# A spectral mix and an attention in one stream of matmuls: maxima ahead by more tiles, keys loaded by head, ones rows sent first

## The chip, the cores and the metric

The kernel runs on one core of a Trainium2 chip. Time is the device time of one execution in microseconds. Within the core, TensorE (PE) multiplies, VectorE (DVE), ScalarE (ACT) and GpSimd (POOL) do the work on vectors, and SyncE (SP) issues most of the copies between memories; POOL issues some too. Each engine takes its instructions in the order in which they are written, and stops at one whose inputs or outputs are not ready. PSUM is the memory into which PE writes, in eight places of 128 x 512 here.

## The reference, cut to what matters

The result mixes two branches row by row, 2048 rows of 512. Branch A is the real part of a two-dimensional Fourier transform, written as products with four given matrices. Branch B is attention with 32 heads of 16 columns.

```
g = sigmoid((x * gate_w).sum(-1))
a = x @ Wd_re.T;  b = x @ Wd_im.T
y = Ws_re @ a - Ws_im @ b
q, k, v = split(x @ wqkv)            # 32 heads of 16
o = softmax(q @ k.T / 4) @ v ;  B = o @ wo
out = g * y + (1 - g) * B
```

## The kernel before

Every float32 factor is split into a high and a low part, so that a product takes three matmuls. The heads are taken in 16 pairs; pair `p` has 32 units `u` (two halves of the queries by 16 blocks of keys), 512 units in all. For a pair, `qs` and `ks` hold q and k of head 0 in the lower 64 partitions and of head 1 in the upper 64, with rows left for a maximum (in `qs`) and for ones (in `ks`): the product of the two then gives the scores with the row's maximum already taken off. There are two `qs` and two `ks`, used by even and odd pairs.

Per unit, PE makes scores (`scores`, L787), ACT their exponentials (L788), PE the product with v (`pv`, L823, and `pv_last`, L804, for the last 16 units). Ahead of that the maxima are needed: `a_tile` makes a product of 128 queries by 512 keys (L247), and DVE takes its largest value (L249); after 64 of these per head a pair's maxima are done, and `m_parts` and `m_rows` write them into `qs`. Tiles are taken head by head: in each head tile `i` of pair `p` goes first over the keys' block 0, for eight blocks of queries (the low half), then over block 1, and so on.

PE works on 64 rows at once in either half, so most work goes in slots of two matmuls: one of branch A or of the projections in one half, one score or maximum in the other. The order of the slots is written out as patterns: `s` a score, `a` a maximum, `d` a product of the other branch alone, a capital letter a second one in the other half, `|` the end of a segment. A segment gives one head its scores, the next the other. At `|` the plan is run (`run_plan`): what was put down with `at(u, ...)` for units up to one beyond those whose values are done is issued there, among it the loads of q and k of the next pair. The segments are 24 THIN, 192 FULL, 2 TWELVE, 30 TEN and 8 at the end.

Before the segments come the projections, v, the imaginary part of A's first product, and then the first real rows, in `four`: four phases of 12 slots, with other work put in behind the slots of some `j` (`between`). There the first maxima are made: `maxima` in the imaginary stage (70 tiles per head, `LEAD`), and `first_tiles` in the stage of the first real rows. The lead is the number of tiles per head that are done when the segments begin; from then on scores and maxima go at the pace of the patterns.

What sets the order around the change: POOL's queue at the start (memsets of `ks`, `qs` and `vt`, and the copies of the rows of ones), SP's queue in the segments (loads of q, `load_q`, whose last copy clears rows of `qs` from a tile of zeros; loads of k in four blocks of 512 keys; copies of A's matrices, `craw`; y, o and r rows to and from memory), and the plan that says after which segment a load is issued.

Of the kernel before, what the change touches and what calls it, by code (L numbers as in the profile page):

```python
# [10 lines left out]
F32 = mybir.dt.float32  # L11
# [5 lines left out]
P = 128  # L17
S = 2048
D = 512
H = 32  # L20
DH = 16
NP = H // 2
KT = D // P
NT = S // P
UNITS = NP * 32
# [7 lines left out]
def mix_kernel(ctx: ExitStack, tc: tile.TileContext, xa_t, xa, wqkv, w_hid, w_seq, wo, gate_w, out):  # L33
# [5 lines left out]
    nc = tc.nc  # L39
# [9 lines left out]
    qk_d = [dram.tile([2, D, S], F32, name=f"qk{c}") for c in range(2)]  # L49
# [29 lines left out]
    def turn_of(kind):  # L79

        group = {"f": banks, "s": banks[:4], "a": [*banks[4:], psD], "r": banks[4:]}[kind]
        turns[kind] += 1
        pool = group[(turns[kind] - 1) % len(group)]
        return pool.tile([P, 512], F32, name="d" if pool is psD else "t")
# [20 lines left out]
    def staged(src):  # L105
        raw = st1.tile([P, D], F32, name="raw", bufs=RAW)
        nc.sync.dma_start(raw, src)
        return raw
# [94 lines left out]
    qs, ks = [None] * 2, [None] * 2  # L203
# [6 lines left out]

    PARTS = (0, 0, 1), (0, 1, 0)

    def load_rows(p, c, cols):


        t = (qs, ks)[c][p % 2]
        rows = slice(2 * p * DH, 2 * (p + 1) * DH)
        for i, v in enumerate(PARTS[c]):
            nc.sync.dma_start(t[i:P:4, cols].bitcast(F32), qk_d[c][v, rows, cols])

    def clear(t, rows, cols):
        dst = t[rows, cols].bitcast(F32).rearrange("r (n c) -> r n c", c=P)
# [3 lines left out]
    def load_q(p, cols):  # L226
        load_rows(p, 0, cols)
        if p > 1:
            clear(qs[p % 2], slice(3, P, 32), cols)
# [8 lines left out]
    def a_tile(i, h, ps=None):  # L238
        p, j = divmod(i, 64)
        n = 4 if p == NP - 1 and j >= 32 else 8  # L240
        k, j = divmod(j, 4 * n)
        kb, qt = divmod(j, n)
        qt += n * k
        if ps is None:
            ps = turn_of("a")
        r = slice(64 * h, 64 * h + 64)
        nc.tensor.matmul(ps, qs[p % 2][r, qt * P:(qt + 1) * P], ks[p % 2][r, kb * 512:(kb + 1) * 512],  # L247
                         start=True, stop=True)
        user = nc.vector.tensor_reduce(mx[p % 2][:, h, qt, kb:kb + 1], ps, AX.X, ALU.max)  # L249
        a_left[p, n, k] = a_left.get((p, n, k), 8 * n) - 1  # L250
        if not a_left[p, n, k]:
            deferred.extend((partial(m_parts, p, n, k), partial(m_rows, p, n, k)))
        return user
# [24 lines left out]
    ones = st1.tile([4, 2 * D], F32, name="hl", bufs=2)  # L278
    nc.gpsimd.memset(ones, 1.0)
    for i in range(2):  # L280
        nc.gpsimd.memset(ks[i].bitcast(F32), 0.0)
        (nc.gpsimd if i else nc.vector).memset(qs[i].bitcast(F32), 0.0)  # L282
        if i == 0:
            load_rows(0, 1, ALL)
            load_q(0, ALL)
            nc.gpsimd.memset(vt[:, :, :, 16:17], 1.0)
        for tb in range(2):
            nc.gpsimd.dma_start(ks[i][3:P:32, tb * 2 * D:(tb + 1) * 2 * D].bitcast(F32), ones)
    wos = [staged(wo[:, kt]) for kt in range(KT)]
    wrs = []  # L290
    a_next = 0
# [3 lines left out]
    def row_products(s, wh, wl):  # L295

        t = ab[s]
        for kt in range(KT):
            hi, lo = (t[:, v, kt * P:(kt + 1) * P] for v in range(2))
            yield from ((hi, wh[kt]), (hi, wl[kt]), (lo, wh[kt]))  # L300
# [24 lines left out]
    def maxima():  # L325

        nonlocal a_next
        users = [a_tile(a_next, h) for h in range(2)]
        a_next += 1
        return users[1]  # L330

    def four(ss, wh, wl, done, between=None):

        ps = [turn_of("s") for _ in ss]
        seen = None
        for phase, pair in enumerate(((0, 1), (2, 3), (1, 0), (3, 2))):
            guard, seen = seen, None
            both = [row_products(ss[c], wh, wl) for c in pair]
            for j in range(12):
                for half, c in enumerate(pair):  # L340
                    st, mv = next(both[half])
                    r = slice(64 * half, 64 * half + 64)
                    i = nc.tensor.matmul(ps[c], st[r], mv[r], start=phase < 2 and j == 0, stop=phase > 1 and j == 11)  # L343
                    if phase > 1 and j == 0:
                        tc.add_manual_dep(
                            i.ins, guard.ins.name,
                            mybir.DependencyInfo(mybir.DependencyClass.Sync, mybir.DependencyReason.DATA))
                if j in (((2, 7), (1, 5, 10), (3, 8), (1, 5, 10))[phase] if not between else (3, 8)):
                    user = between(phase, j) if between else maxima()
                    seen = seen or user  # L350
            if deferred:
                deferred.pop(0)()
            if phase > 1:
                for c in sorted(pair):
                    done(ss[c], ps[c])
# [55 lines left out]
    def bank(i=None):  # L411

        nonlocal now
        if i is None:
            i = min(range(7), key=lambda j: free[j])
        now = max(now, free[i] + 0.7)
        return i, banks[i].tile([P, 512], F32, name="t")

    def read_by(i, kind):

        nonlocal dve, act
        if kind == "a":
            dve = max(now + 2.0, dve) + 2.6
            free[i] = dve + 0.4
        else:
            act = max(now + 2.0, act) + 2.1
            free[i] = act + 0.5
# [345 lines left out]
    def scores(u, qb, h, ps=None):  # L773
        p, r = divmod(u, 32)
        hf, kt = divmod(r, 16)
        q0 = hf * 1024 + qb * 512
        if u >= UNITS - 16:

            blk, kt = divmod(kt, 8)
            q0, kt = 1024 + blk * 512, 2 * kt + qb  # L780
        if u not in pts:
            pts[u] = work.tile([P, 4, 512], F32, name="pt", bufs=4)
        if ps is None:
            i, ps = bank()
            read_by(i, "s")
        rr = slice(64 * h, 64 * h + 64)
        nc.tensor.matmul(ps, ks[p % 2][rr, kt * P:(kt + 1) * P], qs[p % 2][rr, q0:q0 + 512], start=True, stop=True)  # L787
        return nc.scalar.activation(pts[u][:, 2 * qb + h], ps, AF.Exp, bias=0.0, scale=DH ** -0.5)  # L788
# [94 lines left out]
    def at(u, f, *args):  # L883
        plan.setdefault(u, []).append(partial(f, *args))

    for p in range(2, NP):
        u = 32 * (p - 1)
        at(u - 14, load_q, p, LOW)
        for kb in range(4):
            at(u - 14 + 4 * kb, load_rows, p, 1, slice(kb * 512, (kb + 1) * 512))  # L890
        at(u - 2, load_q, p, HIGH)

    for hf in range(2):
        for ct in range(4):
            n = 3 if hf and ct == 3 else 4
# [28 lines left out]

    FULL = "s a s s a a s s a a s a s a a s |"
    THIN = "aS s a s a s s a s a s a a sA |"
    TWELVE = ("sA a s a s ^ s a s a s s a s |",) * 2
    TEN = "aA s s a s ^ s s s a a sS |", "a s a sS a ^ s s s s s aA |"

    def stream(h):  # L930

        return (
            iter([(u, qb, h) for u in range(UNITS) for qb in range(2)]),
            iter([(i, h) for i in range(lead, NP * 64)]),
        )

    streams = [stream(h) for h in range(2)]

    users, valued = [], 0
# [66 lines left out]
    def pairs():  # L1006

        for i in range(NT - 4):
            yield (THIN,) * 2, take(hid, 12)
        for i in range(2 * NT * 3):  # L1010
            yield (FULL,) * 2, take(seq, 16)
        for patterns, n in ((TWELVE, 1), (TEN, 15)):
            for i in range(n):
                yield patterns, take(both_first, 9)

# [13 lines left out]

    def first_tiles(phase, j):  # L1030

        if j == 3:
            user = scores(*next(streams[0][0]), turn_of("r"))
            a_tile(*next(streams[1][1]), turn_of("r"))
            return user
        for h in range(2):
            a_tile(*next(streams[h][1]), turn_of("r"))

    four(range(4), *wre, first_rows, first_tiles)
    free[:] = 0.0, 0.0, 4.0, 4.0, 1.0, 2.0, 3.0  # L1040
    hid, seq = real(), dft()
# [10 lines left out]
    for hf, qts in ((1, range(2)), (1, range(2, 5)), (1, range(5, 8)), (0, range(2))):  # L1052
        for half in range(2):
            ds = take(proj(hf, (3,), [held_bank] * (len(qts) - 1) + one, qts, half == 1), 9, False)
            if valued < UNITS - 12:
                pattern = TEN[half]
            else:
                pattern = "s s ^ s s s s s s |" if len(qts) < 3 else "s s ^ s s d s s s s |"
                if valued == UNITS - 2:
                    pattern = "s s s s d d |"  # L1060
            segment(pattern, half, ds, True, after.get(valued), False)
    assert not any(a_left.values())
    last_pair(last)
# [36 lines left out]
```

## Time and profile before

| | |
|---|---|
| median of 3 runs | 1669.23 us (1668.42 to 1669.26) |
| profiled execution | 1669.81 us |
| its span | 1667.9 us |
| PE busy | 1658.0 us, 99% |
| DVE busy | 1374.9 us, 82% |
| ACT busy | 1251.0 us, 75% |
| POOL busy | 753.4 us, 45% |

How to read it: the page lists busy time per engine, the span in 40 slices, the queues of copies, the chain of work that ended last, and the groups of instructions. A row of a timeline gives the start in us, the length in us, the engine, the line of the kernel, the operation, the tiles written and read, the shapes and a count; in brackets stands how long the engine was idle ahead of it, and what ended that. SPq and POOLq are copies at their issue; the length there is that of the issue and not of the transfer.

### The profile page before, as it was taken

Reading aid. Unit: us, or ns where it says so; the run is one execution under the profiler, and the core shown is the slowest. Engines: PE = TensorE matmul, PEld = TensorE weight load, DVE = VectorE, ACT = ScalarE, POOL = GpSimd, SP = SyncE. Lnnn points to the kernel's source line nnn. Section 1 sums busy time; section 2 is a strip of 40 time slices with the busy share of each in tenths; the row PEclk is TensorE's granted clock in tenths of the full one; section 3 lists DMA queues with packets and bytes.
Section 4 is the critical chain, followed back from the end, with each engine's and each line's share of the span. In section 5 each row is a group of like instructions: output and inputs, shape, how many; then the busy total and the mean of one; then the engine's idle time right before and its main releaser. Section 6 shows DMA issues by size and latency. Waiting matters only on the chain.

```text
span 1667.9 us, 34971 instructions
## 1 busy us (share of the span) xinstructions
PE 1658.0 (99%) x13170; PEld 984.6 (59%) x13170; DVE 1374.9 (82%) x2283; ACT 1251.0 (75%) x2486; POOL 753.4 (45%) x813
## 2 busy tenths in 40 slices
PE   9999999999999999999999999999999999999998
PEld 7878866655555555555555555555555555555554
DVE  5459988888888888888888888888888888877786
ACT  5212188887777788877777788877778788799995
POOL 0223643544454455544444465554545566333331
PEclk9999999999999999999999999999999999999999
DMA  9953301122221224222127224322222333451114
GB/s 295 342 156 132 151 21 38 29 59 60 71 70 51 63 80 130 73 65 65 54 76 263 79 84 122 95 76 67 71 65 68 92 97 117 149 194 43 26 48 134
DMA packets 90176, 165.65 MB, mean 99 GB/s; under 512 B 21056, under 2 KB 22472, under 8 KB 88856
## 3 DMA queue, kind: packets, MB, share of 16 engines
q1 hardware_dynamic: 85368, 162.63, 31.2%
q8 instruction: 104, 1.70, 0.4%
q0 software_dynamic: 4352, 0.39, 0.2%
q14 instruction: 64, 0.52, 0.1%
q10 hardware_dynamic: 288, 0.39, 0.1%
HBM read 107.73 MB, written 54.52 MB: 97 GB/s over the span
## 4 chain that ended last, share of the span: by engine, by line
PE 98%; DVE 0%; POOL 0%; DMA 0%; issue 0%; SPq 0%; DVEq 0%; ACT 0%
PE d L456 37%; PE t L823 28%; PE t L247 12%; PE t L787 9%; PE t L343 5%; PE t L93 2%; PE t L92 2%; PE t L91 2%; PE t L804 1%; PE t L456 1%; DMA ks<-qk 0%; PE t L161 0%; PE t L183 0%; DVE mx L249 0%; DVE yp L648 0%; PE t L733 0%
## 5 line engine op out<-in xcount | busy, mean ns | idle before, releaser
L249 DVE TENSOR_REDUCE mx<-t 128x1 f32<-128x512 f32 x2013 | 1253.2, 683 | 226.8 <-PE t L247 192.3
L788 ACT ACTIVATE pt<-t 128x512 f32<-128x512 f32 x2048 | 1033.5, 632 | 10.5 <-PE t L787 9.3
L787 PE MATMUL t<-qs,ks 64*128 64x512 f32 x2048 | 728.7, 408 | 0.4 <-DVE mx L249 0.2
L247 PE MATMUL t<-ks,qs 64*128 64x512 f32 x2013 | 675.6, 399 | 1.6 <-POOL qs L282 1.6
L456 PE MATMUL d<-xab,ch 64*128 64x512 f32 x2016 | 656.5, 400 | 0.0
L823 PE MATMUL t<-pt,vt 128*32 128x512 f32 x3968 | 477.1, 598 | 0.0
L456 PEld LDWEIGHTS d<-xab,ch 64*128 64x128 f32 x2016 | 357.8, 184 | 142.2 <-issue 98.1
L247 PEld LDWEIGHTS t<-ks,qs 64*128 64x128 f32 x2013 | 359.8, 184 | 84.2 <-ACT pt L788 55.9
L787 PEld LDWEIGHTS t<-qs,ks 64*128 64x128 f32 x2048 | 367.0, 184 | 71.3 <-DVE mx L249 40.8
L456 PE MATMUL d<-xab,cl 64*128 64x512 f32 x1008 | 403.4, 400 | 0.0
L838 POOL TENSOR_TENSOR osum<-osum,oe 128x512 f32<-128x512 f32 x217 | 279.6, 1289 | 161.7 <-ACT oe L832 153.8
L832 ACT COPY oe<-t 128x512 f32<-128x512 f32 x217 | 127.4, 587 | 215.5 <-PE t L823 213.8
L823 PEld LDWEIGHTS t<-pt,vt 128*32 128x32 f32 x3968 | 103.6, 109 | 232.1 <-issue 148.7
L401 POOL CAST ch<-craw 128x512 fp32r<-128x512 f32 x126 | 77.3, 613 | 348.4 <-PE t L787 322.7
L456 PEld LDWEIGHTS d<-xab,cl 64*128 64x128 f32 x1008 | 185.8, 184 | 72.3 <-issue 50.3
L402 POOL TENSOR_TENSOR cl<-craw,ch 128x512 fp32r<-128x512 f32 x126 | 162.3, 1288 | 10.2
L270 POOL DMA_DIRECT2D qs<-mt x132 | 73.6, 562 | 90.4 <-DVE mt L266 80.1
L456 PE MATMUL d<-wo_hl,o_hl 64*128 64x512 f32 x288 | 75.3, 395 | 0.0
L456 PE MATMUL d<-wre,xab 64*128 64x512 f32 x288 | 70.3, 389 | 0.0
L456 PEld LDWEIGHTS d<-wo_hl,o_hl 64*128 64x128 f32 x288 | 51.8, 184 | 17.4 <-ACT pt L788 12.6
L456 PEld LDWEIGHTS d<-wre,xab 64*128 64x128 f32 x288 | 52.8, 184 | 3.1
L91 PE MATMUL t<-xab,wh 128*128 128x512 f32 x124 | 48.2, 389 | 0.0
(118 smaller groups left out, 935.8 us busy)
## 6 DMA issues: line engine op xcount, KB each, us to landing
craw<-w_seq SPq DMA_DIRECT2D x128, 256.0 KB
qk<-hl SPq DMA_DIRECT2D x32, 512.0 KB
qs<-qk SPq DMA_DIRECT2D x84, 128.0 KB
ks<-qk SPq DMA_DIRECT2D x168, 64.0 KB
b<-hl SPq DMA_DIRECT2D x16, 512.0 KB
xab<-b SPq DMA_DIRECT2D x16, 512.0 KB
o<-osum SPq DMA_DIRECT2D x62, 128.0 KB
oh<-nh SPq DMA_DIRECT2D x12, 512.0 KB
```

Source lines behind the costliest of these rows:

```text
L91: nc.tensor.matmul(ps, sh, mh, start=first, stop=False)
L247: nc.tensor.matmul(ps, qs[p % 2][r, qt * P:(qt + 1) * P], ks[p % 2][r, kb * 512:(kb + 1) * 512], start=True, stop=True)
L249: user = nc.vector.tensor_reduce(mx[p % 2][:, h, qt, kb:kb + 1], ps, AX.X, ALU.max)
L343: i = nc.tensor.matmul(ps[c], st[r], mv[r], start=phase < 2 and j == 0, stop=phase > 1 and j == 11)
L401: nc.gpsimd.tensor_copy(h1, raw)
L402: nc.gpsimd.tensor_tensor(l1, raw, h1.bitcast(F32), ALU.subtract)
L456: i = nc.tensor.matmul(self.ps, st[r], mv[r], start=not self.begun, stop=stop)
L787: nc.tensor.matmul(ps, ks[p % 2][rr, kt * P:(kt + 1) * P], qs[p % 2][rr, q0:q0 + 512], start=True, stop=True)
L788: return nc.scalar.activation(pts[u][:, 2 * qb + h], ps, AF.Exp, bias=0.0, scale=DH ** -0.5)
L823: nc.tensor.matmul(acc[32 * j:32 * j + 32], vt[:, kt, p, h:h + 32], pt[:, j], start=u == us[0], stop=u == us[-1])
L832: nc.scalar.copy(oe, acc)
L838: nc.gpsimd.tensor_tensor(o, o, oe, ALU.add)
```

## The change

Five things are changed.

1. The copies of the rows of ones into `ks` stand right behind the memset of their `ks`, ahead of the memset of `vt`. For the second pair, `qs` is cleared ahead of `ks`.
2. In the first real rows, work of the attention is put in at three places of a phase (behind slots 2, 6 and 10) and no longer at two (3 and 8). In the first three phases its results go to the four PSUM places of the maxima ("a"), in the last to three ("r"). The lead becomes 78 tiles for head 0 and 82 for head 1, from 74 and 78.
3. `load_rows` can load one head alone. For pairs 3 to 14, k of head 1 is loaded two units (one segment) earlier than k of head 0, in each of four blocks.
4. The two segments TWELVE become EVEN, with 12 slots each in place of 13 and ten maxima in place of twelve.
5. The first two of the last eight segments take the pattern of eight scores, and no longer TEN with its maxima.

```diff
-    def load_rows(p, c, cols):
+    def load_rows(p, c, cols, heads=(0, 1)):
         t = (qs, ks)[c][p % 2]
-        rows = slice(2 * p * DH, 2 * (p + 1) * DH)
+        h0, h1 = heads[0], heads[-1] + 1
+        rows = slice((2 * p + h0) * DH, (2 * p + h1) * DH)
         for i, v in enumerate(PARTS[c]):
-            nc.sync.dma_start(t[i:P:4, cols].bitcast(F32), qk_d[c][v, rows, cols])
+            nc.sync.dma_start(t[64 * h0 + i:64 * h1:4, cols].bitcast(F32), qk_d[c][v, rows, cols])
...
     for i in range(2):
+        (nc.gpsimd if i else nc.vector).memset(qs[i].bitcast(F32), 0.0)
         nc.gpsimd.memset(ks[i].bitcast(F32), 0.0)
-        (nc.gpsimd if i else nc.vector).memset(qs[i].bitcast(F32), 0.0)
+        for tb in range(2):
+            nc.gpsimd.dma_start(ks[i][3:P:32, tb * 2 * D:(tb + 1) * 2 * D].bitcast(F32), ones)
         if i == 0:
             load_rows(0, 1, ALL)
             load_q(0, ALL)
             nc.gpsimd.memset(vt[:, :, :, 16:17], 1.0)
-        for tb in range(2):
-            nc.gpsimd.dma_start(ks[i][3:P:32, tb * 2 * D:(tb + 1) * 2 * D].bitcast(F32), ones)
...
-                if j in (((2, 7), (1, 5, 10), (3, 8), (1, 5, 10))[phase] if not between else (3, 8)):
+                if j in (((2, 7), (1, 5, 10), (3, 8), (1, 5, 10))[phase] if not between else (2, 6, 10)):
...
         at(u - 14, load_q, p, LOW)
         for kb in range(4):
-            at(u - 14 + 4 * kb, load_rows, p, 1, slice(kb * 512, (kb + 1) * 512))
+            cols = slice(kb * 512, (kb + 1) * 512)
+            if 2 < p < NP - 1:
+                at(u - 16 + 4 * kb, load_rows, p, 1, cols, (1,))
+                at(u - 14 + 4 * kb, load_rows, p, 1, cols, (0,))
+            else:
+                at(u - 14 + 4 * kb, load_rows, p, 1, cols)
         at(u - 2, load_q, p, HIGH)
...
-    TWELVE = ("sA a s a s ^ s a s a s s a s |",) * 2
+    EVEN = "aA s s a s ^ s d s sA a d sS |", "a s a sS a ^ s a s s s s a |"
...
     def first_tiles(phase, j):
-        if j == 3:
-            user = scores(*next(streams[0][0]), turn_of("r"))
-            a_tile(*next(streams[1][1]), turn_of("r"))
+        kind = "r" if phase == 3 else "a"
+        if j == 2:
+            user = scores(*next(streams[0][0]), turn_of(kind))
+            a_tile(*next(streams[1][1]), turn_of(kind))
             return user
         for h in range(2):
-            a_tile(*next(streams[h][1]), turn_of("r"))
+            a_tile(*next(streams[h][1]), turn_of(kind))
...
-            if valued < UNITS - 12:
-                pattern = TEN[half]
-            else:
-                pattern = "s s ^ s s s s s s |" if len(qts) < 3 else "s s ^ s s d s s s s |"
-                if valued == UNITS - 2:
-                    pattern = "s s s s d d |"
+            pattern = "s s ^ s s s s s s |" if len(qts) < 3 else "s s ^ s s d s s s s |"
+            if valued == UNITS - 2:
+                pattern = "s s s s d d |"
```

The lines from 213 on move by one or more in the changed kernel: L247 becomes L248, L787 L788, L823 L824, L804 L805.

On SP, in the segments ahead of pair 6, where `ks_937` and `qs_936` are that pair's tiles (k and q of the even pairs). Before:

```order
L601 DMA oh_142<-nh 256x1x512
L841 DMA o_104<-osum 64x512 x2
L581 DMA no<-o_105 64x1x512
L584 DMA no<-r_152 64x1x512
L581 DMA no<-o_105 64x1x512
L584 DMA no<-r_152 64x1x512
L391 DMA craw<-w_seq 128x512
L219 DMA qs_936<-qk_86 32x1024 x3
L224 DMA qs_936<-zero 4x8x128
L219 DMA ks_937<-qk_87 32x512 x3
```

And after the change:

```order
L602 DMA oh_142<-nh 256x1x512
L842 DMA o_104<-osum 64x512 x2
L220 DMA ks_937<-qk_87 16x512 x3
L582 DMA no<-o_105 64x1x512
L585 DMA no<-r_152 64x1x512
L582 DMA no<-o_105 64x1x512
L585 DMA no<-r_152 64x1x512
L392 DMA craw<-w_seq 128x512
L220 DMA qs_936<-qk_86 32x1024 x3
L225 DMA qs_936<-zero 4x8x128
L220 DMA ks_937<-qk_87 16x512 x6
```

Three copies of head 1's k, a segment earlier, now stand ahead of the loads of q; q and its clear are where they were among the rest.

On PE, the end of the segment behind the one that issues this load of q; `ks_939` is pair 5's k, and the words in brackets are the semaphores that the matmul waits on (DMAHW for copies of SP). Before:

```order
L787 MATMUL t<-qs_936,ks_937 128x512 [waits DVE_49]
L456 MATMUL d<-xab_179,ch 128x512
L247 MATMUL t<-ks_939,qs_938 128x512 [waits Activation_49]
L456 MATMUL d<-xab_179,cl 128x512
L247 MATMUL t<-ks_939,qs_938 128x512 [waits Activation_49]
L456 MATMUL d<-xab_179,ch 128x512 x2
L787 MATMUL t<-qs_936,ks_937 128x512 [waits DVE_49]
```

And after:

```order
L788 MATMUL t<-qs_936,ks_937 128x512 [waits DVE_49]
L457 MATMUL d<-xab_179,ch 128x512
L248 MATMUL t<-ks_937,qs_936 128x512 [waits DMAHW3_49,DMAHW2_49,DMAHW4_49,DMAHW1_49,Activation_49]
L457 MATMUL d<-xab_179,cl 128x512
L248 MATMUL t<-ks_937,qs_936 128x512 [waits Activation_49]
L457 MATMUL d<-xab_179,ch 128x512 x2
L788 MATMUL t<-qs_936,ks_937 128x512 [waits DVE_49]
```

The last two maxima of this segment were still those of pair 5; now they are the first two of head 1 of pair 6, and the first of them waits on copies.

On POOL, the start of the attention; `ks_937` is pair 0's k, `ks_939` and `qs_938` pair 1's, `hl` the tile of ones. Before:

```order
L279 MEMSET hl 4x1024
L281 MEMSET ks_937 128x2048
L286 MEMSET vt 128x256
L288 DMA ks_937<-hl 4x1024 x2
L281 MEMSET ks_939 128x2048
L282 MEMSET qs_938 128x2048
L288 DMA ks_939<-hl 4x1024 x2
```

And after:

```order
L280 MEMSET hl 4x1024
L283 MEMSET ks_937 128x2048
L285 DMA ks_937<-hl 4x1024 x2
L289 MEMSET vt 128x256
L282 MEMSET qs_938 128x2048
L283 MEMSET ks_939 128x2048
L285 DMA ks_939<-hl 4x1024 x2
```

The two copies of pair 0's ones have moved ahead of the memset of `vt`.

More of the change, by code (lines that the diff above doesn't have):

```diff
@@ L1011, in pairs @@
             yield (FULL,) * 2, take(seq, 16)
-        for patterns, n in ((TWELVE, 1), (TEN, 15)):
+        for patterns, n in ((EVEN, 1), (TEN, 15)):
             for i in range(n):
```

## The prediction

> **What bounds the kernel now.** I read the page's first, second and fourth parts (busy times, slices, chain), the list of waits of TensorE (PE), and then the timelines of PE, GpSimd (POOL), VectorE (DVE) and SyncE (SP) at the places that the change touches.
>
> ```profile
> span 1667.9 us, 34971 instructions
> PE 1658.0 (99%) x13170; PEld 984.6 (59%) x13170; DVE 1374.9 (82%) x2283; ACT 1251.0 (75%) x2486; POOL 753.4 (45%) x813
> ...
> PEclk9999999999999999999999999999999999999999
> ...
> PE 98%; DVE 0%; POOL 0%; DMA 0%; issue 0%; SPq 0%; DVEq 0%; ACT 0%
> ```
>
> PE is busy 99% of the span, carries 98% of the chain that ended last, and has the full clock throughout. So a slot of PE that is added or removed shows at once, and so does any time in which PE's next instruction is not ready; DVE at 82% is the one neighbour close enough to matter. The change issues the same number of matmuls in all, so only waits and slots with one half empty can move the time. The profiled execution is the span and 1.9 us around it, 1669.81 us; the median of the runs is 0.6 below, 1669.23. A measurement here can tell about 0.2%, 3.3 us, from no change.
>
> **Ones rows first.** PE has one gap here.
>
> ```profile
> 104.40 0.96 PE L343 MATMUL t<-wv,xab 64*128 64x512 f32 x6
> 106.93 0.50 PE L247 MATMUL t<-ks,qs 64*128 64x512 f32 x2 [1.57 <-POOL qs L282]
> ...
> 93.42 1.81 POOL L281 MEMSET ks<- 128x2048 f32 x1 [40.67 <-PE t L92]
> 100.75 0.59 POOL L286 MEMSET vt<- 128x256 f32 x1 [5.52 <-DMA ks<-qk]
> 101.27 1.28 POOL L288 DMA_DIRECT2D ks<-hl  x2
> 104.30 1.83 POOL L282 MEMSET qs<- 128x2048 f32 x1
> ...
> DMA to landing us min/median/max: 2.1/3.7/5.5
> ```
>
> The name behind the gap is the last POOL work that had ended, the memset at 104.30, but that one clears pair 1's tile, which this matmul doesn't read. What it reads of POOL's is pair 0's rows of ones, issued at 101.27 behind the vt memset, and with the slowest landing of the last row, 5.5, they come at 106.8. After the change they are issued where the ks memset ends, 93.42 + 1.81 = 95.2, and even 5.5 later land at 100.7. PE's matmuls ahead of it end near 105.3, so the gap of 1.57 goes, with its pipeline refill about 1.7. The two memsets of pair 1 that change places aren't read before pair 1's first maximum, a whole stage later. I take **−1.7**, of 0 (something else was also late) to −1.8.
>
> **First real rows, three places.** The four phases hold 3 × 2 scores or maxima each in place of 2 × 2: four more PE slots. The tiles wait for DVE.
>
> ```profile
> 202.23 1.75 PE L343 MATMUL t<-wre,xab 64*128 64x512 f32 x14
> 203.82 0.39 PE L787 MATMUL t<-qs,ks 64*128 64x512 f32 x1
> ...
> 201.19 0.74 DVE L766 TENSOR_SCALAR ng<-ng 128x16 f32<-128x16 f32 x1 [0.25 <-ACT ng L765]
> 202.47 2.55 DVE L249 TENSOR_REDUCE mx<-t 128x1 f32<-128x512 f32 x4
> 214.06 3.08 DVE L249 TENSOR_REDUCE mx<-t 128x1 f32<-128x512 f32 x5 [0.22 <-PE t L247]
> ```
>
> Seven slots take 203.82 − 202.23, so a slot is 0.228, and four are +0.91. DVE works off a tile every 0.60 (five in 3.08, the last one 0.68 long), and before 202.47 it is held by the gate's five small operations. From these I laid out the stage by hand: PE reaches the fifth tile of the phases at about 202.7, but its PSUM place was that of the first, whose reduction begins only at 202.47 and releases at 203.2: 0.5 lost. Within a phase five tiles take DVE 3.0 of 15 × 0.228 = 3.4, so waits there are small (0.2 in all). The last phase returns from four places to three and finds one still being read: 0.6. That is 0.9 + 0.5 + 0.2 + 0.6, with rounding **+2.3**; 0.9 if DVE keeps up, 2.9 if one more place is found taken.
>
> **Lead 78 and 82, and what must then be there.** With eight more tiles done by the first rows, head 1 reaches a pair's first maximum nearly two segments earlier: in FULL, in the 14th slot of the segment after the one that ends with `load_q(p, LOW)`, instead of the sixth slot two segments on. That matmul reads head 1's q, the cleared rows and the first block of k. The change moves k for head 1 forward by a segment, but q LOW and its clear stay, and the three new k copies now stand ahead of them in SP's queue.
>
> ```profile
> 356.71 0.66 SPq L224 DMA_DIRECT2D qs<-zero  x1
> ...
> 450.80 0.33 SPq L511 DMA_DIRECT2D yr<-y  x1
> 451.70 1.75 SPq L219 DMA_DIRECT2D qs<-qk  x3
> 453.63 0.66 SPq L224 DMA_DIRECT2D qs<-zero  x1
> ...
> 632.35 1.18 SPq L841 DMA_DIRECT2D o<-osum  x2
> 636.79 1.76 SPq L219 DMA_DIRECT2D qs<-qk  x3
> 638.73 0.66 SPq L224 DMA_DIRECT2D qs<-zero  x1
> 639.49 1.74 SPq L219 DMA_DIRECT2D ks<-qk  x3
> ...
> 732.28 0.66 SPq L224 DMA_DIRECT2D qs<-zero  x1
> ...
> 915.89 0.67 SPq L224 DMA_DIRECT2D qs<-zero  x1
> ```
>
> The five clears are those of pairs 3, 4, 6, 7 and 9. In the same segments the slot that will hold the first tile starts, today, at these times:
>
> ```profile
> 361.49 0.39 PE L247 MATMUL t<-ks,qs 64*128 64x512 f32 x1
> 454.44 0.40 PE L247 MATMUL t<-ks,qs 64*128 64x512 f32 x1
> 640.23 0.40 PE L247 MATMUL t<-ks,qs 64*128 64x512 f32 x1
> 733.11 0.39 PE L247 MATMUL t<-ks,qs 64*128 64x512 f32 x1
> 919.30 0.39 PE L247 MATMUL t<-ks,qs 64*128 64x512 f32 x1
> ...
> qs<-mt POOLq DMA_DIRECT2D x124, 2.0 KB, 1.7
> ```
>
> A landing of SP's copies has no row. The nearest are 1.7 for 2 KB on POOL's queue and, above, 2.1 at best and 3.7 in the middle for 16 KB of ones, the clear's size, all from the issue. I take 1.8 from the end of the clear's issue (2.5 from its start), since three copies of 128 KB go just ahead of it.
> - Pair 4: SP waits at 450.80 for the y store, which ScalarE (ACT) releases, so the k copies slip in before it at no cost: 454.29 + 1.8 − 454.44 = 1.65.
> - Pair 6: SP comes late out of the o store, which POOL releases, and is without a gap from there, so three more copies push by 1.74 (the row at 639.49): 639.39 + 1.74 + 1.8 − 640.23 = 2.7.
> - Pair 7, again behind a y store: 732.94 + 1.8 − 733.11 = 1.6.
> - Pair 9, pushed: 916.56 + 1.74 + 1.8 − 919.30 = 0.8.
> - Pair 3, pushed: 357.37 + 1.74 + 1.8 = 360.9, in time by 0.6. The same working leaves pairs 10, 12 and 14 in time by about 1, 13 by 1.3, and 5, 8 and 11 by 3 or more.
>
> Together **+6.8**. While PE waits, DVE and ACT run dry, and as PE is the bound nothing is made up. Counting landings from the issue, 1.7 gives 0.9 + 1.9 + 0.9 + 0.0 = 3.7, and 3.7 about 13, with pairs 3, 10, 12 and 14 late as well; a gain is excluded, as the wait only adds. 1.8 lies nearest the best landing, since the queues are otherwise quiet here.
>
> [...]
>
> The split k adds 12 pairs × 4 blocks × 3 = 144 copies at 0.58, 84 us of SP's time; SP has long gaps, and the k blocks themselves are wanted 2.5 us or more after they land, so they cost nothing beyond the push above. If that cover went, the second k block would be late next.
>
> **EVEN for TWELVE, and the end.** PE's first value products of these segments:
>
> ```profile
> 1460.40 0.64 PE L823 MATMUL t<-pt,vt 128*32 128x512 f32 x4
> 1470.72 0.64 PE L823 MATMUL t<-pt,vt 128*32 128x512 f32 x4
> ...
> 1614.90 0.64 PE L823 MATMUL t<-pt,vt 128*32 128x512 f32 x4
> 1619.29 0.64 PE L804 MATMUL t<-pt,vt 128*32 128x512 f32 x4
> 1624.82 0.64 PE L804 MATMUL t<-pt,vt 128*32 128x512 f32 x4
> 1643.74 0.64 PE L804 MATMUL t<-pt,vt 128*32 128x512 f32 x4
> 1647.96 0.64 PE L804 MATMUL t<-pt,vt 128*32 128x512 f32 x4
> ...
> 1621.95 4.03 ACT L788 ACTIVATE pt<-t 128x512 f32<-128x512 f32 x8 [0.37 <-PE t L456]
> ```
>
> TWELVE's two segments took 10.32 with 13 slots each; EVEN has 12, two slots of 0.228 fewer: **−0.4** (0 to −0.5). The two segments behind TEN lose their six maxima and become eight slots each. They took 4.39 and 5.53. An eight-slot segment of today took 4.22, and ACT needs 4.03 + 0.37 = 4.40 for its eight exponentials; two such are 8.8, so **−1.1**, of 0 (if the products before them bind) to −1.5. The remaining maxima finish earlier, so their rows have more time.
>
> **Sum.** −1.7 + 2.3 + 6.8 − 0.4 − 1.1 = +5.9 on 1669.81, 1675.7, and against the median 1669.23 + 5.9 = **1675.1 us**, 0.35% slower.
>
> **Rivals.**
> - q LOW is in time after all. It needs the clear landed by the slot, for pair 6 within 0.84 of its present issue end and before any push; pairs 5, 8 and 11 show that SP can be 3 us sooner, but in pairs 4, 6, 7 and 9 the y and o stores hold it. Then −1.7 + 2.3 − 0.4 − 1.1 = −0.9: 1668.3, within 0.2%. 17%.
> - The other side: DVE keeps up in the first rows, at 0.9, and q is in time; with the ends of the other terms, −1.8 + 0.9 − 0.5 − 1.5 = −2.9: 1666.3. It passes the bound of −3.3 only where the wider first rows also relieve the THIN stage behind them. The point that decides is the waits for q: below 0.0 in total it can be faster. DVE's start at 202.47 speaks against it. 6%.
> - SP slips further. Pairs 3, 10, 12 and 14 are within 1 us of being late; 0.8 more of landing time makes all of them wait a little and adds 0.8 to the four: +3.5, so 1678.6. 9%.
> - The clock drops. Pair 6's wait is the longest idle time of PE; the gaps of today, at most 1.57, left the clock at 9 in every slice. If half the clock were granted for as long again as such a wait, 2.7, it would cost 1.35 more: 1676.5. 3%. [...]
>
> **How the numbers follow.** The forecast holds 65%, 1671.8 (landings at 1.7) to 1677. Behind it stand 9 + 3% above, 17 + 6% below. The range takes in the rival with q in time and that with SP further behind: 1667.8 to 1679.0. Slower by over 0.2% (above 1672.6): most of 65 (62) and 12, 74%; faster (below 1665.9): 4%; the rest, 22%, within 0.2%.
>
> **What would show it.** Right: no gap at the first L248; PE idle before L248 near 454, 640, 733 and 919 us, put down to a DMA or to whatever ended last, up to 2.7 long; DVE without gaps from 202.5 to 216; the span from the first segment to the last otherwise as now. Wrong: L248 without idle time in FULL, which would mean SP reached q LOW earlier than its rows of today say, or k blocks named as late.

## The result

The changed kernel takes 1678.9 us in the median of four runs (1676.71 to 1679.52), against 1669.1 (1668.42 to 1669.26) for the kernel before it: a ratio of 1.0057, 95% interval 1.004 to 1.0075, slower by 9.8 us. The profiled execution has a span of 1676.4, 8.5 more than before. Outside the span, every kernel here whose k is split spends 2.1 to 2.4 us in each of its executions, and every other 1.8 to 1.9: some 0.3 of the difference is there, and the traces, which hold the span alone, do not show why. The forecast was 1675.1 in a range of 1667.8 to 1679.0, slower with a chance of 0.74.

The page of the changed kernel:

```profile
span 1676.4 us, 35226 instructions
PE 1659.6 (99%) x13170; PEld 991.0 (59%) x13170; DVE 1375.9 (82%) x2283; ACT 1252.2 (75%) x2486; POOL 753.5 (45%) x813
...
PEclk9999999999999999999999999999999999999999
...
PE 97%; DMA 1%; DVE 1%; SPq 1%; ACT 0%; issue 0%; DVEq 0%; ACTq 0%
...
L248 PE MATMUL t<-ks,qs 64*128 64x512 f32 x2009 | 674.1, 398 | 8.6 <-DMA qs<-zero 3.6
```

PE does the same work as before, to 1.6 us, with the full clock. What is new is idle time ahead of the maxima's matmuls, 8.6 us, and copies on the chain that ended last, which was PE's to 98% before.

Copies and waits at the start, POOL first and then PE:

```profile
92.84 1.81 POOL L283 MEMSET ks<- 128x2048 f32 x1 [40.46 <-PE t L92]
94.96 1.29 POOL L285 DMA_DIRECT2D ks<-hl  x2 [0.31 <-POOL ks L283]
100.08 0.58 POOL L289 MEMSET vt<- 128x256 f32 x1 [3.83 <-issue]
...
104.61 0.40 PE L248 MATMUL t<-ks,qs 64*128 64x512 f32 x2
```

The ones are issued at 94.96 in place of 101.27, and the first maximum's matmul, at 104.61, has no idle time ahead of it.

In the first real rows, PE:

```profile
202.08 0.44 PE L248 MATMUL d<-ks,qs 64*128 64x512 f32 x1
203.03 0.67 PE L248 MATMUL t<-ks,qs 64*128 64x512 f32 x2
...
208.91 0.50 PE L788 MATMUL t<-qs,ks 64*128 64x512 f32 x1
209.51 0.49 PE L248 MATMUL t<-ks,qs 64*128 64x512 f32 x1
```

At 208.91 to 209.51 two matmuls of one slot stand 0.60 apart: the turn back from four PSUM places to three, which finds its place in use (with four places, in e8_four_places below, both start at 208.21).

In FULL, the clear of q's rows at its issue on SP, for pairs 4, 6, 7, 9 and 10, and the first matmul that reads them on PE:

```profile
453.95 0.66 SPq L225 DMA_DIRECT2D qs<-zero  x1
642.84 0.66 SPq L225 DMA_DIRECT2D qs<-zero  x1
737.88 0.66 SPq L225 DMA_DIRECT2D qs<-zero  x1
925.10 0.67 SPq L225 DMA_DIRECT2D qs<-zero  x1
1017.40 0.66 SPq L225 DMA_DIRECT2D qs<-zero  x1
...
456.62 0.46 PE L248 MATMUL t<-ks,qs 64*128 64x512 f32 x1 [1.64 <-DMA ks<-qk]
549.70 0.47 PE L248 MATMUL t<-ks,qs 64*128 64x512 f32 x1
645.77 0.46 PE L248 MATMUL t<-ks,qs 64*128 64x512 f32 x1 [2.95 <-DMA qs<-zero]
740.66 0.46 PE L248 MATMUL t<-ks,qs 64*128 64x512 f32 x1 [1.75 <-DMA ks<-qk]
927.53 0.47 PE L248 MATMUL t<-ks,qs 64*128 64x512 f32 x1 [0.61 <-DMA qs<-zero]
1021.62 0.46 PE L248 MATMUL t<-ks,qs 64*128 64x512 f32 x1 [1.00 <-ACT pt L789]
```

The names behind the gaps are not to be taken at their word. At 456.62 and 740.66 the page names a copy of k, which for this matmul had long been there: the next k copies are only issued from 454.71 and 738.64 on, and are not read by it. In pairs 4, 6, 7 and 9 the matmul starts 1.8 to 2.3 after the end of its clear's issue, in pair 10 3.6 after. At 549.70, pair 5, the copies had been there for 3 us, and there is no gap in the row.

The first value products of segments, at EVEN and at the end:

```profile
1470.56 0.64 PE L824 MATMUL t<-pt,vt 128*32 128x512 f32 x4
1480.34 0.64 PE L824 MATMUL t<-pt,vt 128*32 128x512 f32 x4
...
1624.82 0.64 PE L824 MATMUL t<-pt,vt 128*32 128x512 f32 x4
1628.91 0.64 PE L805 MATMUL t<-pt,vt 128*32 128x512 f32 x4
1633.23 0.64 PE L805 MATMUL t<-pt,vt 128*32 128x512 f32 x4
```

From the starts of the same matmuls in the two traces, the difference of the spans divides as follows. "Before the attention" ends where POOL clears pair 0's `ks`; that comes at 92.8 to 93.4 in the eleven traces, with the change and without it, so its row is taken for no part of the change.

| stretch | forecast | measured |
|---|---|---|
| before the attention | | −0.6 |
| ones rows first | −1.7 | −1.8 |
| first real rows | +2.3 | +2.2 |
| THIN and FULL (the waits for q, and all else there) | +6.8 | +10.3 |
| EVEN | −0.4 | −0.5 |
| TEN | 0 | +0.3 |
| the two eight-score segments | −1.1 | −1.5 |
| behind them | 0 | +0.1 |
| sum | +5.9 | +8.5 |

Segment by segment, what THIN and FULL gained stands in the segments in which head 1 reaches a new pair: 0.50 for pair 3, 1.88 for pair 4, 0.18 for 5, 3.23 for 6, 1.97 for 7, 0.17 for 8, 0.85 for 9, 1.25 for 10, 0.19 for 11, 0.30 for 12, less than 0.1 for 13 and 0.36 for 14: 10.9. Two other segments, in which the kernel before lost 0.28 each, lose nothing now.

### The profile page after: what moved, and what is told of

Read it like the earlier page. It is cut to its first block, busy times and chain, and to the rows that moved or that the text cites. A ratio compares the mean times of both kernels' runs of the same rounds, so it can differ in the third digit from the quotient of the medians.

```text
span 1676.4 us, 35226 instructions
## 1 busy us (share of the span) xinstructions
PE 1659.6 (99%) x13170; PEld 991.0 (59%) x13170; DVE 1375.9 (82%) x2283; ACT 1252.2 (75%) x2486; POOL 753.5 (45%) x813
## 4 chain that ended last, share of the span: by engine, by line
PE 97%; DMA 1%; DVE 1%; SPq 1%; ACT 0%; issue 0%; DVEq 0%; ACTq 0%
PE d L457 36%; PE t L824 27%; PE t L248 11%; PE t L788 10%; PE t L344 5%; PE t L92 2%; PE t L93 2%; PE t L91 2%; PE t L805 1%; PE t L457 1%; PE t L362 1%; PE d L248 0%; SPq L220 0%; DMA ks<-qk 0%; DVE mx L250 0%; DMA qs<-zero 0%
## 5 line engine op out<-in xcount | busy, mean ns | idle before, releaser
L788 PE MATMUL t<-qs,ks 64*128 64x512 f32 x2048 | 728.4, 409 | 0.2
L248 PE MATMUL t<-ks,qs 64*128 64x512 f32 x2009 | 674.1, 398 | 8.6 <-DMA qs<-zero 3.6
L824 PE MATMUL t<-pt,vt 128*32 128x512 f32 x3968 | 477.1, 598 | 0.0
L248 PEld LDWEIGHTS t<-ks,qs 64*128 64x128 f32 x2009 | 358.5, 184 | 85.4 <-ACT pt L789 50.5
L788 PEld LDWEIGHTS t<-qs,ks 64*128 64x128 f32 x2048 | 366.6, 184 | 69.6 <-DVE mx L250 40.0
L824 PEld LDWEIGHTS t<-pt,vt 128*32 128x32 f32 x3968 | 103.6, 109 | 232.1 <-issue 150.5
```

What stands on the lines that cost most here:

```text
L824: nc.tensor.matmul(acc[32 * j:32 * j + 32], vt[:, kt, p, h:h + 32], pt[:, j], start=u == us[0], stop=u == us[-1])
```

## The experiments

Theory W: the loss is PE waiting for the low half of q, whose load stands where it stood while its first reader came forward. Rival S: it is SP's 144 more copies, and the work that they hold up. In FULL, segments are compared one by one with the kernel before; an undisturbed one takes 5.81 us.

**q loaded a segment earlier** (e1_q_early): the changed kernel with

```diff
-        at(u - 14, load_q, p, LOW)
+        at(u - (16 if 2 < p < NP - 1 else 14), load_q, p, LOW)
```

> The changed kernel with q LOW and its clear of pairs 3 to 14 loaded a segment earlier (ahead of head 1's k). Theory W (PE waits for q LOW in eight pairs, 10 to 11 us in all): these waits go, FULL is at 5.81 us a segment in every segment, and the time falls by 8.5 to 10.5 to 1668.5 to 1670.5. Rival S (SP's 144 more copies are what costs): the copies are all still there, at least half of the excess stays, 1674 or more.

Measured: 1669.89 us (before, on the same chip, 1668.61; ratio 1.0009, 1.0000 to 1.0018). Some 8.5 of the 9.8 us are gone with one line, and all 144 copies are still there. PE's list of waits no longer has L248 in it:

```profile
PE t L161 <- DVE zero L60: 1.1, 1, 1.1
PE t L183 <- ACT xab L87: 0.6, 1, 0.6
```

W holds, and S as the main cause falls. But one part of W's expectation failed: not every segment went to 5.81. The twelve in which head 1 reaches a new pair take 5.97 to 6.02, 0.16 to 0.21 more each, 2.2 us in all, though q had landed 1.7 us or more before. That became theory E, below.

**Only the split of k** (e2_split_only), on the kernel before:

```diff
-            at(u - 14 + 4 * kb, load_rows, p, 1, slice(kb * 512, (kb + 1) * 512))
+            cols = slice(kb * 512, (kb + 1) * 512)
+            if 2 < p < NP - 1:
+                at(u - 16 + 4 * kb, load_rows, p, 1, cols, (1,))
+                at(u - 14 + 4 * kb, load_rows, p, 1, cols, (0,))
+            else:
+                at(u - 14 + 4 * kb, load_rows, p, 1, cols)
```

> The kernel before with k of head 1 loaded by itself a segment earlier, and nothing else of the change (lead 74 and 78 as before). W: q LOW is pushed by up to 1.7 us but has 8 us or more of room, so 1669.1, within 1 us. S: slower by 4 us or more.

Measured: 1668.43 (0.9999, 0.9990 to 1.0007). By themselves the copies cost nothing that the times can tell: no segment of THIN and FULL is longer by 0.05 or more, and the 0.3 outside the span is offset by what the span gains. They do push q: here, too, SP comes without a gap from head 1's k to q, and the copies of q start 5.0 after those of k:

```profile
632.50 1.81 SPq L220 DMA_DIRECT2D ks<-qk  x3
...
637.54 1.76 SPq L220 DMA_DIRECT2D qs<-qk  x3
639.47 0.65 SPq L225 DMA_DIRECT2D qs<-zero  x1
```

With the old lead q is not read until two segments later. The two segments at 6.09 of the kernel before are at 5.81 here, and at 6.09 again in e4_q_early_k_whole, which has no split; so that small gain belongs to the split. What brings it is not shown.

**Only the ones first** (e3_ones_only), on the kernel before: the two copies moved as in the change.

```diff
         nc.gpsimd.memset(ks[i].bitcast(F32), 0.0)
+        for tb in range(2):
+            nc.gpsimd.dma_start(ks[i][3:P:32, tb * 2 * D:(tb + 1) * 2 * D].bitcast(F32), ones)
```

> The kernel before with only the copies of the ones moved ahead of the vt memset. If the start is worth what the two profiles show (1.84), 1667.3 (1666.9 to 1667.9); if what it gains is lost again in the stages behind, 1669.1.

Measured: 1667.4 (1667.1 to 1667.68) against 1668.61; ratio 0.9992, 0.9984 to 1.0001. That is 1.2 of the expected 1.8, and the interval just takes in no change. In the profile the gap at the first maximum is gone and the first value products start at 215.03 and not at 216.92, so it is kept to there.

**Why k was split** (e4_q_early_k_whole): q early, but k of both heads at the old place.

```diff
-            if 2 < p < NP - 1:
+            if False:
                 at(u - 16 + 4 * kb, load_rows, p, 1, cols, (1,))
```

> e1_q_early with k of both heads loaded together in the old place, one segment behind q LOW, so that the 144 copies more are not there. W with the same reading for k (head 1's first maximum of each block comes 14 slots into the segment behind the load): waits of 0.3 to 2 us for k in a good part of the 48 blocks, 3 to 12 us slower than e1_q_early, named as DMA ks<-qk. Rival: k is in time anyway and the split is not needed: within 1 us of e1_q_early.

Measured: 1685.49 (1.0108, 1.0092 to 1.0123), 15.6 above e1_q_early: the right sign and more than the 3 to 12 expected. In its profile 15 segments lose 0.4 to 2.8 each, nine of them where a later block of k than the first is read; the list of waits has 12 stops:

```profile
PE t L248 <- DMA ks<-qk: 10.4, 12, 2.6
```

So the longer lead needs head 1's k earlier, which the split gives, and q would have needed the same (loading k of both heads a segment earlier was not tried): the change moved one of the two things that the earlier reader reads.

**The gate behind the first real rows** (e5_gate_late), on e1_q_early:

```diff
     run_plan(0)
-    gate()
+    at(16, gate)
```

> e1_q_early with the gate's operations on ScalarE and VectorE moved from ahead of the first real rows to behind the eighth segment. If VectorE's late start at 202.5 costs PE 0.5 in the first real rows, 0.4 to 0.9 below e1_q_early, with no new wait in THIN; if VectorE then falls behind in THIN, the same or above.

Measured: 1669.93, no different from e1_q_early by times. In the profiles the stretch from the maximum at the start of the first real rows to the first value products is 0.5 shorter (20.7 in place of 21.3), the size that the prediction gave this wait, and no segment of THIN differs from e1_q_early by more than 0.02. Half a microsecond is below what the runs can tell.

**Theory E: the waits as instructions** (e6_waits_early). In e1_q_early the data are there, yet these matmuls are late. Ahead of the matmul the trace has four semaphore instructions on PE's queue of weight loads. The rows of the maxima's line, in e1_q_early around pair 3's first tile and in the kernel before around its own:

```profile
L248 PEldq EVENT_SEMAPHORE  x4: 51/51/51, 361.3 to 361.6; - x4
```

```profile
L247 PEldq EVENT_SEMAPHORE  x4: 51/51/51, 369.3 to 369.7; - x4
```

In the kernel before, they run at 369.3 to 369.7, within the value products, which fill 368.1 to 370.0; their reader is at 371.2. In e1_q_early they run at 361.3 to 361.6, in the middle of the slots, and the next two matmuls are 0.35 apart in place of 0.23:

```profile
361.34 0.42 PE L788 MATMUL t<-qs,ks 64*128 64x512 f32 x1
...
361.69 0.47 PE L248 MATMUL t<-ks,qs 64*128 64x512 f32 x1
```

Amid the slots a weight load begins one slot, 0.23, ahead of its matmul; in the last of the value products the queue of weight loads is idle for 0.84 while PE still works on them. Rows of the kernel before, PE first and then its weight loads:

```profile
798.69 1.04 PE L823 MATMUL t<-pt,vt 128*32 128x512 f32 x8
...
800.70 0.39 PE L247 MATMUL t<-ks,qs 64*128 64x512 f32 x1
...
799.66 0.18 PEld L456 LDWEIGHTS d<-xab,ch 64*128 64x128 f32 x1 [0.84 <-issue]
...
800.47 0.18 PEld L247 LDWEIGHTS t<-ks,qs 64*128 64x128 f32 x1
```

To test whether the four instructions are what makes the matmul late, the waits were put on the first matmul of the segment, behind the value products. For that the copies must land earlier, so q LOW went another segment ahead.

```diff
+            at(u - 18, noted, p, load_q, p, LOW)          # notes the copies that are issued
...
+                    for d in early.pop(valued, ()):
+                        tc.add_manual_dep(i.ins, d.ins.name, ...)   # i: first matmul of the segment
```

> e5_gate_late with q LOW another segment earlier and PE's waits on these copies (q, clear, first block of k) put on the first matmul of the segment, behind the value products, and no longer on the 14th slot. Theory E (in e1_q_early each of the twelve first maxima costs 0.17 us though its data are there, because PE executes four semaphore instructions 0.11 us apart with only one slot of weights loaded ahead): all segments of FULL at 5.81, 2.0 us less than e5_gate_late. Rival: the 0.17 belongs to the first reading of a new tile: the twelve segments stay at 5.98, no change.

Measured: 1670.13, no gain in time. But in ten of the twelve segments the 0.17 is gone (they differ from the kernel before by 0.01 or less). The two others took the gain back: pair 9's by 1.86 and pair 3's by 0.36, where head 1's first k, which was waited for in the new place too, had not landed yet.

```profile
PE d L462 <- DMA ks<-qk: 1.8, 1, 1.8
```

E is borne out, its rival is not: the same tiles are read for the first time at the same slot, without the loss.

**Four places in the last phase of the first real rows** (e8_four_places), on e6_waits_early:

```diff
-        kind = "r" if phase == 3 else "a"
+        kind = "a"
```

> e6_waits_early with four PSUM places for the maxima in the last phase of the first real rows too. If the turn back to three places is what costs 0.6 in that phase, 0.5 less than e6_waits_early in the first real rows; but the fourth place is also that of the first chain of THIN, and if that chain then waits for VectorE, the gain is lost there. In sum 1666 to 1667, below the kernel before by 1.5 to 2.5.

Measured: 1669.5 (1.0007, 0.9998 to 1.0016), not the 1666 to 1667 that was expected. In its profile (1670.19) pair 9's segment alone takes 3.8 more: PE stops for 2.25 at head 1's k, and then its granted clock is 0.50 for 3.4 us, which makes up the other 1.5 (start and end, length, busy time of PE, its weight loads, DVE, ACT and POOL with their instructions, granted clock, share and rate of the copies):

```profile
917.07:920.20 3.13, 3.13 (x15) 2.66 (x17) 1.29 (x2) 1.68 (x3) 0.00 (x0) 0.50 0.33 83
```

In the first real rows the gain is the expected 0.5 (17.7 from the first score to the first value products, 18.1 in e6_waits_early), though the first chain of THIN does stop for VectorE at the fourth place, for 1.0:

```profile
PE d L462 <- DMA ks<-qk: 2.3, 1, 2.3
PE t L161 <- DVE zero L60: 1.1, 1, 1.1
PE d L462 <- DVE mx L255: 1.0, 1, 1.0
```

**Only q's waits early** (e9_q_waits_early), on e8_four_places, with k waited for where it is read:

```diff
-                if kb:
-                    at(u - 16 + 4 * kb, load_rows, p, 1, cols, (1,))
-                else:
-                    at(u - 16, noted, p, load_rows, p, 1, cols, (1,))
+                at(u - 16 + 4 * kb, load_rows, p, 1, cols, (1,))
```

> e8_four_places with only the waits on q LOW and its clear on the first matmul of the segment; head 1's k is waited for where it is read. Theory: the two stops of 2.3 and 0.2 us at head 1's k (pairs 9 and 3) go, and three semaphore instructions at the 14th slot cost at most 0.1 in each pair: 2 to 3 us less than e8_four_places, 1665.5 to 1667.5, 1 to 3 us below the kernel before. Rival: k is late at the 14th slot too: no gain on e8_four_places.

Measured: 1666.82 (1666.2 to 1667.2) against 1668.77; ratio 0.9988, 0.9979 to 0.9997. This is the changed kernel with q two segments earlier, its waits moved, the gate late and four places throughout; it is faster than the kernel before by 2 us or 0.12%, and the interval just leaves out no change. Pair 9 still loses 0.32, and no other pair more than 0.03, although the waits for head 1's k are left at the 14th slot, as two semaphore instructions there:

```profile
L253 PEldq EVENT_SEMAPHORE  x2: 51/51/51, 1382.7 to 1382.8; - x2
```

**The yardstick** (e10_ones_gate): the kernel before, with the ones first and the gate late.

> The kernel before with only the ones sent first and the gate moved behind the eighth segment: 0 to 0.4 below e3_ones_only's difference to before (1.2), so 1667.0 to 1667.6; it is the yardstick for what the changed order of maxima is worth beside the start.

Measured: 1667.21 (0.9991, 0.9982 to 1.0000). e9_q_waits_early is 0.4 below it, and the intervals overlap: what the new order of the maxima brings beside the start can't be told from nothing.

## Why the prediction was right, and where its sizes were off

- **The number.** 1678.9 is in the range by 0.1 only, and two of the four executions (1679.23, 1679.52) are not. It lies above the 1671.8 to 1677 that was given 65%. The range reached this far for the rival with SP slipping further, of which only part came true (below), so that it held is in part luck.
- **Direction and mechanism.** Slower, because head 1's first maximum waits for q LOW: shown by the gaps in the rows at the forecast slots (pairs 4, 6, 7, 9), and by e1_q_early, which removes them with the load alone.
- **Ones first, −1.7:** measured −1.84 in the traces and 1.2 in the medians of e3_ones_only. From the start of the six matmuls ahead of the gap to the first maximum's matmul it was 2.53 us before (104.40 to 106.93) and is 0.80 now (103.81 to 104.61): 1.73 less, 0.16 beyond the idle 1.57, where the prediction put about 0.1 for the refill.
- **First real rows, +2.3:** measured +2.24 (the four parts as given add up to 2.2). The parts that were named were seen too: e5_gate_late gave back 0.5 for the gate, e8_four_places 0.5 for the turn to three places.
- **EVEN −0.4 and the end −1.1:** −0.54 and −1.51. The eight-score segments take 4.09 and 4.32, below the 4.40 that was worked out from ScalarE's row, so the 0.37 of idle time that was counted with ScalarE's 4.03 was not needed; whether ScalarE bounds these segments is not shown.
- **The waits for q, +6.8, is the term that was mis-sized:** the segments of the twelve pairs gained 10.9. Of the 4.1 more, 2.2 is the price of the waits themselves, which the sum had at nothing: it is what these segments lose in e1_q_early, where nothing is late (0.16 to 0.21 each; in the changed kernel it stands by itself in pairs 5, 8 and 11). With that taken off, pairs 4, 6, 7 and 9 were late by 7.2 against 6.8, and pairs 3, 10, 12 and 14, which had been put in time, by 1.7, of which pair 10 is 1.1.
- **What held in it.** SP's side: pair 6's clear ends its issue at 643.50, the forecast being 639.39 + 1.74, and 2.4 for what PE had lost by then, 643.53. The landing too, taken as 1.8 from the end of the clear's issue: by the trace's semaphore events it was 1.77, 2.13, 1.88 and 1.64 for pairs 4, 6, 7 and 9, and the matmul started 0.13 to 0.25 after that. In the kernel before, the 24 clears took 1.62 to 2.05. From the start of their issue the clears of the twelve pairs here took 2.27 to 2.79, against the 2.5 of the prediction. The queues were less quiet than it had them: from 631 to 645 the kernel before has a DMA share of 0.57.
- **Pair 10** had been put in time by about 1 and lost 1.25. Its clear landed at 1020.04, within 2 us, but two of the pieces of q issued ahead of it only at 1021.2 and 1021.5; the prediction had followed the clear alone.
- **The rivals.** q in time (17%) is answered by the rows, VectorE keeping up in the first real rows (6%) by their +2.24. SP slipping further (9%) came nearest in size, but what made pair 10 late is the landing of q and not SP. The clock (3%) stayed full in the profiled execution of the change, after its stop of 2.95; but in e8_four_places it fell after a stop of 2.25, and cost 1.5, near this rival's 1.35. The two longest executions of the change have a mean granted clock of 0.998, as has that profile of e8_four_places, and the two others 0.999; whether the clock fell in them is not shown, as they left no trace.

## What to carry to other kernels

When work is moved ahead, every input that it reads has to move with it: here k was moved and q was not, and one line was worth 8.5 us. On an engine that is busy 99% of the time, the room of each load is read from its issue to the slot of its new first reader, pair by pair, with the queue in front of it. Copies that are issued together are all to be followed to their landing, since the last to be issued need not be the last to land: pair 10's clear landed at 1020.04, and two pieces of q issued ahead of it at 1021.2 and 1021.5. Waits had a price of their own here, 0.16 to 0.21 us at a matmul with four semaphore instructions ahead of it amid the slots; it fell to 0.01 or less where they stood on an earlier matmul behind the value products, and to 0.03 or less with two in place of four.

## What the runs showed of the hardware

In e1_q_early a matmul's waits cost PE 0.16 to 0.21 us although q had landed 1.7 us or more before. For the seven copies that head 1's first maximum waits on (three of q, the clear, three of k), its trace shows four semaphore instructions of 0.05 us, 0.11 apart, on PE's queue of weight loads, amid slots of two matmuls. Two of them at the same slot cost 0.03 or less (e9_q_waits_early, all pairs but 9), and three or four behind a block of 16 value products 0.01 or less (e6_waits_early, ten segments). That the loads run only one slot, 0.23 us, ahead amid the slots, and that their queue is idle for 0.84 us in the last of the value products (the rows under theory E), fits this; that it is what hides the instructions there is argued from it, and not shown by itself.

The landing of three copies of 128 KB issued one behind another varied: by the trace's semaphore events the last was there 2.2 us after SP was done with them for pair 4, and 4.3 for pair 10, where 15 of its 16 events had come by 1019.6 and the last at 1021.5.

In these runs the length of a gap alone does not tell whether PE's granted clock falls. Those of 2.95 (the changed kernel, pair 6) and 2.56 (e4_q_early_k_whole, pair 6) left it at 1.00. The one of 2.25 in e8_four_places was followed by 3.4 us at 0.50, with 15 matmuls in the 3.13 us shown above, against 26 in the 3.30 us behind pair 6's wait in the changed kernel, in the same form of table:

```profile
645.70:649.00 3.30, 3.23 (x26) 1.40 (x28) 1.29 (x2) 0.87 (x2) 0.00 (x0) 1.00 0.14 35
```
